# A long convolution and a segmented attention on one core: keys as eight token classes, paired taps in four blocks, gate factors as value columns, the memory's sum in PSUM, and a new order

## The chip, the cores and the metric

The kernel runs on one core of one Trainium2 chip. The metric is the device time of one execution in microseconds (us), as the median of several. A profile is one execution, taken apart instruction by instruction. The engines are TensorE (PE, whose weight loads are listed apart as PEld), VectorE (DVE), ScalarE (ACT) and GpSimd (POOL); SyncE (SP) issues nearly all DMAs, in the order of its program.

## The reference

Two independent layers read their own inputs, and their outputs stand side by side in a [2048, 1280] result.

Layer A works on 2048 tokens and 640 channels. The key is filtered along the tokens with four taps per channel, the result is multiplied by the value, convolved causally with a filter as long as the sequence, and multiplied by the query:

```
k_shift = sum over t of k_pad[:, t:t + S, :] * shift_k[:, 3 - t]
kv = k_shift * v
y = causal convolution of kv with ssm_k (by FFT), + kv * ssm_D
a = q * y
```

Layer B projects x with three 640 x 640 matrices to 32 heads of 20 columns and works on four segments of 512 tokens in turn. In each, causal softmax attention inside the segment is mixed, by a gate per head, with a read from a memory that earlier segments wrote:

```
a_dot = softmax(qs @ ks.T * scale + mask) @ vs
a_mem = phi(qs) @ M / (phi(qs) @ z + 1e-6)
o = g * a_mem + (1 - g) * a_dot,  with g = sigmoid(beta)
M = M + phi(ks).T @ vs;  z = z + sum of phi(ks)
```

The output is `o @ wo`. phi(t) is t + 1 above zero and exp(t) below.

## The kernel before

**Layer A** is five blocks of 128 channels (`conv(dp)`). A block loads its long filter (`load_filter`), loads and filters the key (`short_filter`), takes both through a transform made of matmuls with the table Wf (`spectrum`, whose PSUM results are copied to the tile F and combined on DVE), multiplies the two spectra on DVE (`product`), and goes back with the table Wi (`inverse`). The tokens stand as eight classes: token 8p + e of a half of 1024 tokens is row p of class e.

The short filter runs on PE. The key block is turned (channels on partitions) by one DMA transpose from DRAM into the tile kr, 16 zero columns ahead of 2048 tokens. The weights of each matmul are 128 of its columns, eight apart (`kr[:, first + m:first + m + 1017:8]`), and the moving operand skd is a matrix with the taps on its diagonal. Blocks 0 and 1 do it with seven matmuls of up to 512 columns for each of four results. Blocks 2 to 4, listed in `TAP2`, pair two taps: with three more DMAs (the step "lc"), kr and a second tile kb each hold 64 channels twice, the second time shifted by two tokens, and ten matmuls of 128 or 64 columns do.

**Layer B** is eight units u: four segments s, each in two halves of 16 heads. `project(u)` makes queries and keys (KQ), turns them by DMA (KQT), makes the values (Va), phi of both (PP, for the queries in two steps of two token tiles each), a bound for the logits that stands in for the row maximum (the tiles kam, A, qabs, bT), and adds the segment to the memory Mbd. `attend(u)` makes the masked logits on PE in four kinds of fills (A, D, J: two exponentials of 128 x 1024 on ACT for each, into ET), and `values` multiplies them with Va. Every head's slot has 22 columns; column 20 of Va holds 1 + exp(beta), so that the column's sum is the softmax's denominator with the factor of the gate in it. Memory's own denominator is multiplied by 1 + exp(-beta) in another way: the update goes through a mask into the tile mt, its column 20 is multiplied by emg, and mt is added to Mbd, three DVE instructions in all. `project_out(s)` multiplies the segment's outputs with wo and stores them.

**The order** is no loop's. `Recorder` collects each operation of the whole program (1543 of them; the matmuls of one PSUM result count as one), and two packed lists at the end of the file, ORDER and BASE, give the sequence in which they are issued and the PSUM bank of each result. Each engine, and SP, runs its part of this list in order and waits on semaphores. All instructions are issued at line 256. `EVICT` says for each of the 238 copies out of PSUM whether ACT or DVE does it. At the start, 20 matmuls on zeros (`WARM`) keep PE busy while the first loads are under way.

Of the kernel before, what the change touches and what calls it, by code (L numbers as in the profile page):

```python
# [13 lines left out]
bf16 = mybir.dt.bfloat16  # L14
f32 = mybir.dt.float32
# [29 lines left out]
def small_consts():  # L45
# [3 lines left out]
    sel = np.zeros((128, 32), np.float32)  # L49
# [4 lines left out]
    for hh in range(4):  # L54
        rows = (hl == hh) & (d < DH)
        maskbd[rows, hh, 0:DH + 1] = 1.0
        epsrow[32 * hh + DH + 1, hh] = EPS
# [207 lines left out]
class Layer:  # L265
    def __init__(self, ctx, tc, A_q, A_k, A_v, A_shift_k, A_ssm_k, A_ssm_D, B_x, B_wq, B_wk, B_wv, B_wo, B_beta, out):
# [14 lines left out]
        self.rings = {}  # L281
# [30 lines left out]
        skr = self.ring("skd", [128, 4, 128])[0:5].rearrange("c a b -> c (a b)")  # L312
# [31 lines left out]
        self.evict(self.taps[:], tp, g)  # L344

# [4 lines left out]
        self.kr = c.tile([128, KPAD + S], bf16, name="kr")  # L350
# [6 lines left out]
        nc.gpsimd.memset(self.kr[:, 0:KPAD], 0.0)  # L357
        self.kb = c.tile([128, KPAD + S], bf16, name="kb")
        nc.gpsimd.memset(self.kb[:, 0:KPAD], 0.0)
# [7 lines left out]
        if WARM:  # L367
# [4 lines left out]
            for n in range(WARM):  # L372
                rec.key = ("warm", n)
                with rec.one():
                    nc.tensor.matmul(g.ap[:, 0, 0:WARMC], lhsT=idle[:, 0:128], rhs=idle[:, 128:128 + WARMC], start=True, stop=True, grp=g)

# [19 lines left out]
    def beta_setup(self):  # L396
        nc, c, bt = self.nc, self.consts, self.bt
        V = nc.vector
        em = c.tile([128, H], f32, name="em")
# [3 lines left out]
        nc.scalar.activation(out=em[:], in_=g.ap[:, 0, 0:H], func=ACTF.Exp, scale=-1.0, grp=g)  # L403
        ep, ginv = [self.ring("rr", [128, 2, 16], f32, n=2)[:].rearrange("p a b -> p (a b)") for _ in range(2)]
        nc.scalar.activation(out=ep, in_=g.ap[:, 0, 0:H], func=ACTF.Exp, grp=g)
        omginv = c.tile([128, H], f32, name="omginv")
        V.tensor_scalar(out=em[:], in0=em[:], scalar1=1e30, scalar2=None, op0=ALU.min)
        V.tensor_scalar(out=ginv, in0=em[:], scalar1=1.0, scalar2=None, op0=ALU.add)
        V.tensor_scalar(out=omginv[:], in0=ep, scalar1=1.0, scalar2=1e30, op0=ALU.add, op1=ALU.min)
        for h in range(2):  # L410
            V.tensor_copy(out=self.Va[h][:, :, :, DH], in_=omginv[:, None, 16 * h:16 * h + 16].to_broadcast([128, 4, 16]))
        self.emg = em[:].rearrange("p (g h) -> p g h", h=4)
        for h in range(2):
            V.tensor_tensor(out=self.Mbd[h][0][:, :, :, DH], in0=ginv[:, 16 * h:16 * h + 16].rearrange("p (g h) -> p g h", h=4),
                            in1=self.epsrow[:, None, :].to_broadcast([128, 4, 4]), op=ALU.mult)

# [11 lines left out]
    def conv(self, dp):  # L428
# [31 lines left out]
        def short_filter():  # L460
            key("lk")
            kr = self.kr
            if dp in KTURN:
                kn = self.ring("ET", [128, 4, 512], n=ETBUF)[:].rearrange("p (b c) (e d) -> p (b c) e d", c=2, e=4)[:].rearrange("p x e d -> p (x e) d")
                for a in range(2):
                    nc.sync.dma_start(out=kn[:, 8 * a:8 * a + 8], in_=self.k[1024 * a:1024 * a + 1024, dsl].rearrange("(p e) d -> p e d", e=8))
                for x in range(4):
                    key("kn", x)
                    g = self.group(1, "kn")
                    with rec.one():  # L470
                        for e in range(4):
                            nc.tensor.matmul(g.ap[:, 0, 128 * e:128 * e + 128], lhsT=kn[:, 4 * x + e], rhs=self.ident[:], start=True, stop=True, grp=g)
                    at = KPAD + 1024 * (x // 2)
                    self.evict(kr[:, at:at + 1024].rearrange("d (p e) -> d e p", e=8)[:, 4 * (x % 2):4 * (x % 2) + 4], g.ap[:, 0, :].rearrange("d (e p) -> d e p", e=4), g)
            else:
              nc.sync.dma_start_transpose(out=kr[:, KPAD:KPAD + S], in_=self.k[:, dsl])
            if dp in TAP2:
# [8 lines left out]
            key("skd")  # L486
            skd = self.ring("skd", [128, 4, 128])
            if dp in TAP2:
                skd2 = skd[:].rearrange("p a d -> p (a d)")[:, 0:256].rearrange("p (f l d) -> p f l d", f=2, l=2)
                V.tensor_tensor(out=skd2, in0=self.id2[:, None, None, :].to_broadcast([128, 2, 2, 64]), in1=self.taps[:, 0:4, dp].rearrange("p (f l) -> p f l", f=2)[:, :, :, None].to_broadcast([128, 2, 2, 64]), op=ALU.mult)  # L490
            else:
                V.tensor_tensor(out=skd[:], in0=self.ident[:, None, :].to_broadcast([128, 4, 128]),
                                in1=self.taps[:, 4:8, dp, None].to_broadcast([128, 4, 128]), op=ALU.mult)
# [471 lines left out]
```

## Time and profile before

| | |
|---|---|
| time, median of 3 runs | 272.57 us (272.38 to 272.6) |
| profiled execution, first to last instruction | 272.0 us |
| PE busy | 260.8 us, 96% |
| PE weight loads busy | 195.4 us, 72% |
| DVE busy | 250.9 us, 92% |
| ACT busy | 248.8 us, 91% |
| DMA packets | 43.74 MB in 126972 packets |

The time outside the span, 0.57 us against the median, is what lies around the profiled instructions and the difference between two executions. Matmuls are pipelined, so a busy PE may still have room; "busy" counts a stretch once where two instructions overlap. The mean duration of a group is that of an instruction by itself, from its start to its end.

### The profile page before, as it was taken

The page shows a single profiled execution, that of the slowest core. Times are in us where ns is not written, and L with a number is a line of the kernel's source. Part 1 is how long each engine was busy: PE and PEld are TensorE (multiplying, and loading weights), DVE is VectorE, ACT ScalarE, POOL GpSimd, SP SyncE. Part 2 cuts the span into 40 slices and gives each one's busy share as a digit, 9 for nine tenths or more (in the row PEclk, how much of TensorE's full clock was granted, in tenths as well). Part 3 has the DMA queues.
Part 4 walks back from the last instruction along what each step waited for, and adds up shares of the span by engine and source line. Part 5 has one row for each costly group of instructions (what it writes and reads, how often), then busy time and mean ns, then how long its engine had stood idle before and what let it go on. Part 6 is the DMA issues. An engine that isn't in the chain of part 4 may idle for free.

```text
span 272.0 us, 10130 instructions
## 1 busy us (share of the span) xinstructions
PE 260.8 (96%) x4368; PEld 195.4 (72%) x4371; DVE 250.9 (92%) x424; ACT 248.8 (91%) x388; POOL 6.9 (3%) x18
## 2 busy tenths in 40 slices
PE   8999999999998999999999999999999989999995
PEld 3879777868766677878676787768677765756783
DVE  0599999999999999999999999999999998999972
ACT  1586799999999999999999999999999998999962
POOL 9100000000000000000000000000000000000000
PEclk9999999999999999999999999999999997999999
DMA  6999399999989599998979599994974081894024
GB/s 166 347 207 243 82 191 225 311 194 172 170 217 201 144 195 195 191 178 159 159 165 190 116 151 226 147 197 65 146 177 82 4 154 27 169 155 90 27 68 133
DMA packets 126972, 43.74 MB, mean 161 GB/s; under 512 B 117339, under 2 KB 124512, under 8 KB 126800
## 3 DMA queue, kind: packets, MB, share of 16 engines
q1 hardware_dynamic: 126768, 42.91, 79.9%
q8 instruction: 34, 0.56, 0.9%
q0 software_dynamic: 160, 0.20, 0.2%
q14 instruction: 10, 0.08, 0.1%
HBM read 14.12 MB, written 7.34 MB: 79 GB/s over the span
## 4 chain that ended last, share of the span: by engine, by line
PE 55%; ACT 33%; issue 6%; DVE 4%; ACTq 0%; DVEq 0%
PE ps L256 55%; ACT ET L256 21%; ACT F L256 4%; ACT KQ L256 3%; ACT PP L256 3%; ACT outb L256 1%; ACT Va L256 1%; DVE F L256 1%; DVE pq L256 1%; DVE Kh L256 1%; ACT bT L256 1%; DVE qabs L256 0%; DVE vt L256 0%; DVE Xh L256 0%; DVE PP L256 0%
## 5 line engine op out<-in xcount | busy, mean ns | idle before, releaser
L256 ACT ACTIVATE ET<-ps 128x1024 bf16<-128x1024 f32 x160 | 160.6, 1102 | 1.9 <-PE ps L256 1.7
L256 PE MATMUL ps<-wqkv,xT 128*128 128x320 bf16 x480 | 76.3, 300 | 0.5 <-ACT ET L256 0.3
L256 PEld LDWEIGHTS <-xT 128*128 128x128 bf16 x640 | 58.1, 98 | 25.7 <-issue 5.2
L256 PE MATMUL ps<-Va,ET 128*128 128x21 bf16 x1280 | 42.4, 172 | 0.3 <-ACT ET L256 0.3
L256 ACT CAST F<-ps 128x512 bf16<-128x512 f32 x69 | 42.0, 687 | 0.3 <-PE ps L256 0.3
L256 PEld LDWEIGHTS <-ET 128*128 128x128 bf16 x1280 | 39.7, 96 | 3.0 <-issue 2.2
L256 PE MATMUL ps<-KQT 32*128 32x128 bf16 (+2 forms) x896 | 34.6, 240 | 1.1 <-ACT ET L256 1.0
L256 PEld LDWEIGHTS <-Wf 128*128 128x128 bf16 x320 | 28.9, 97 | 6.1 <-issue 1.5
L256 ACT CAST KQ<-ps 128x320 bf16<-128x320 f32 x61 | 28.2, 496 | 1.4 <-PE ps L256 1.3
L256 PE MATMUL ps<-wo,xT 128*128 128x320 bf16 x160 | 25.4, 299 | 0.0
L256 PEld LDWEIGHTS <-KQT 32*128 32x128 bf16 x896 | 16.0, 92 | 10.9 <-issue 9.9
L256 PE MATMUL ps<-vt,Wf 128*128 128x256 bf16 x160 | 22.4, 272 | 0.1
L256 PE MATMUL ps<-kT,Wf 128*128 128x256 bf16 x160 | 22.2, 273 | 0.2 <-ACT ET L256 0.2
L256 PE MATMUL ps<-Y,Wi 128*128 128x256 bf16 x160 | 21.7, 280 | 0.0
L256 DVE TENSOR_TENSOR o<-ps,rr 128x640 bf16<-128x640 f32 x24 | 19.5, 814 | 0.2
L256 PE MATMUL ps<-Mbd,PqT 128*128 128x84 bf16 x96 | 18.1, 202 | 1.2 <-ACT ET L256 0.9
L256 DVE TENSOR_TENSOR Y<-Y,pq 128x2048 bf16<-128x2048 bf16 (+1 forms) x20 | 18.6, 945 | 0.0
L256 DVE TENSOR_TENSOR pq<-Xh,Kh 128x2048 bf16<-128x2048 bf16 x15 | 18.1, 1209 | 0.0
L256 PEld LDWEIGHTS <-Wi 128*128 128x128 bf16 x160 | 15.3, 100 | 3.5 <-issue 1.0
L256 ACT ACTIVATE PP<-KQ 128x640 bf16<-128x640 bf16 (+1 forms) x18 | 17.7, 991 | 0.0
L256 PE MATMUL ps<-pack 32*128 32x128 bf16 x512 | 14.7, 216 | 1.9 <-ACT ET L256 1.7
L256 ACT CAST Va<-ps 128x320 bf16<-128x320 f32 x31 | 15.0, 520 | 1.2 <-PE ps L256 1.2
(93 smaller groups left out, 370.0 us busy)
## 6 DMA issues: line engine op xcount, KB each, us to landing
vt<-in_A_v_dram SPq DMA_DIRECT2D x10, 256.0 KB
pq<-in_A_q_dram SPq DMA_DIRECT2D x10, 256.0 KB
out_dram<-outb SPq DMA_DIRECT2D x13, 160.0 KB
turned<-kT SPq DMA_DIRECT2D x4, 512.0 KB
kT<-turned SPq DMA_DIRECT2D x8, 256.0 KB
out_dram<-pq SPq DMA_DIRECT2D x8, 256.0 KB
kb<-kr SPq DMA_DIRECT2D x6, 256.0 KB
Wf<-c_wf SPq DMA_DIRECT2D x4, 256.0 KB
```

What stands on the lines that cost most here:

```text
L256: f(*[fix(a) for a in args], **{k: fix(v) for k, v in kw.items()})
```

## The change

- **Keys.** kr and kb become [128, 8, 16 + 256] tiles: class e of the eight, then its tokens. In the `TAP2` blocks the key is loaded into kb as it lies in DRAM (two DMAs), turned from there into kr by two DMA transposes inside the chip, and paired by five copies instead of three. The weights of a matmul are then 128 columns that lie side by side. Block 0 keeps the transpose from DRAM and its strided weights.
- **Paired taps** in blocks 1 to 4. The tap matrices of blocks 0 to 2 are made at the start (`filter_weights`), the ring skd has two smaller tiles.
- **Gate.** Va has column 0 for 1 + exp(beta) and column 21 for 1 + exp(-beta), the values stand in columns 1 to 20. The memory's denominator is column 21.
- **Memory's sum.** A further matmul, of the identity with the old Mbd, adds it to the update in PSUM; one DVE instruction masks the sum into the new Mbd.
- **Smaller steps.** phi of the queries in one step of four tiles; the tile A with 4 columns instead of 32 per group; in the first segment two groups of heads share a reciprocal and a multiply; the final add writes runs of 80.
- **Lists.** `WARM` is 10, `EVICT` gives 38 copies to DVE instead of 31, and ORDER and BASE are new, with 1510 operations.

```diff
-            V.tensor_copy(out=self.Va[h][:, :, :, DH], in_=omginv[:, None, 16 * h:16 * h + 16].to_broadcast([128, 4, 16]))
+            some = og[:, :, 16 * h:16 * h + 16]
+            V.tensor_copy(out=self.Va[h][:, :, :, 0:VW:DH + 1], in_=some.rearrange("p i h -> p h i")[:, None].to_broadcast([128, 4, 16, 2]))
...
         def short_filter():
...
-              nc.sync.dma_start_transpose(out=kr[:, KPAD:KPAD + S], in_=self.k[:, dsl])
...
+            flat = kb[:].rearrange("p e n -> p (e n)")
+            if dp in TAP2:
                 for a in range(2):
+                    rows = flat[:, 1024 * a:1024 * a + 1024]
+                    nc.sync.dma_start(out=rows.rearrange("p (e d) -> p e d", e=8), in_=self.k[1024 * a:1024 * a + 1024, dsl].rearrange("(p e) d -> p e d", e=8))
+                for a in range(2):
+                    key("kx", a)
+                    nc.sync.dma_start_transpose(out=kr[:, :, KPAD + 128 * a:KPAD + 128 * a + 128], in_=flat[:, 1024 * a:1024 * a + 1024])
                 key("lc")
                 q = self.queue("lc", dp)
-                q.dma_start(out=self.kb[64:128, KPAD:KPAD + S], in_=kr[64:128, KPAD:KPAD + S])
-                q.dma_start(out=self.kb[0:64, KPAD:KPAD + S], in_=kr[64:128, KPAD - 2:KPAD + S - 2])
-                q.dma_start(out=kr[64:128, KPAD:KPAD + S], in_=kr[0:64, KPAD - 2:KPAD + S - 2])
+                q.dma_start(out=kb[64:128], in_=kr[64:128])
+                q.dma_start(out=kb[0:64, 2:8], in_=kr[64:128, 0:6])
+                q.dma_start(out=kb[0:64, 0:2, KPAD - 1:], in_=kr[64:128, 6:8, KPAD - 2:-1])
+                q.dma_start(out=kr[64:128, 2:8], in_=kr[0:64, 0:6])
+                q.dma_start(out=kr[64:128, 0:2, KPAD:], in_=kr[0:64, 6:8, KPAD - 1:-1])
...
+            def tokens(kx, a, e):
+                at = KPAD + 128 * a - (e < 0)
+                return kx[:, e % 8, at:at + 128]
...
-            for i, n in ((0, 4), (1, 2)):
+            for i, n in ((0, 4), (1, 4)):
...
-        A = self.ring("A", [128, 4, 32], n=1)
+        A = self.ring("A", [128, 4, 4], n=1)
...
-                        nc.tensor.matmul(pmv[:, k, :, 0:DH + 1], lhsT=PP[:, 0, t, 4 * k:4 * k + 4, :], rhs=Va[:, t, 4 * k:4 * k + 4, 0:DH + 1],
-                                         start=(t == 0), stop=(t == 3), grp=g)
-            mt = self.ring("mt", [128, 4, 4, VW])
-            V.tensor_tensor(out=mt[:, :, :, 0:DH + 1], in0=pmv[:, :, :, 0:DH + 1], in1=self.maskbd[:, None, :, 0:DH + 1].to_broadcast([128, 4, 4, DH + 1]), op=ALU.mult, grp=g)
-            V.tensor_tensor(out=mt[:, :, :, DH], in0=mt[:, :, :, DH], in1=self.emg[:, 4 * half:4 * half + 4, :], op=ALU.mult)
-            V.tensor_tensor(out=dst[:, :, :, 0:DH + 1], in0=src[:, :, :, 0:DH + 1], in1=mt[:, :, :, 0:DH + 1], op=ALU.add)
+                        nc.tensor.matmul(pmv[:, k, :, 1:VW], lhsT=PP[:, 0, t, 4 * k:4 * k + 4, :], rhs=Va[:, t, 4 * k:4 * k + 4, 1:VW],
+                                         start=(k == 0 and t == 0), stop=False, grp=g, skip_group_check=True)
+                nc.tensor.matmul(pmv[:, :, :, 1:VW], lhsT=self.ident[:], rhs=src[:, :, :, 1:VW], start=False, stop=True, grp=g, skip_group_check=True)
+            V.tensor_tensor(out=dst[:, :, :, 1:VW], in0=pmv[:, :, :, 1:VW], in1=self.maskbd[:, None, :, 1:VW].to_broadcast([128, 4, 4, DH + 1]), op=ALU.mult, grp=g)
...
+        def values(pp, parts):
+            for j in range(2):
+                if s or not j:
+                    g = self.group(2, "o")
+                weighted(2 * pp + j, *parts[j], g, 0 if s else j)
+                if s == 0 and j == 0:
+                    continue
...
-WARM, WARMC = 20, 512
+WARM, WARMC = 10, 512
...
-TAP2 = (2, 3, 4)
+TAP2 = (1, 2, 3, 4)
```

What the new lists move, read from them. **Start:** SP loads one tile of x ahead of the long filter of block 0, which came first before; seven of the ten matmuls on zeros stand ahead of the first turning of that filter (18 of 20 before), the other three between the transforms that follow. **SP:** 198 DMAs instead of 181; in each paired block the loads of the key stand 1 to 14 places ahead of its transposes, and these up to 14 places ahead of the copies. **EVICT:** DVE takes three more copies of values, two more of KQ, two more of the last turning, one more of the output, and one less of F; the last eight output copies are all DVE's (three before). **End:** the last logits, the last inverse transforms and the 24 last output steps stand as before.

More of the change, by code (lines that the diff above doesn't have):

```diff
@@ L461, in short_filter @@
             key("lk")
-            kr = self.kr
-            if dp in KTURN:
-                kn = self.ring("ET", [128, 4, 512], n=ETBUF)[:].rearrange("p (b c) (e d) -> p (b c) e d", c=2, e=4)[:].rearrange("p x e d -> p (x e) d")
+            kr, kb = self.kr, self.kb
+            flat = kb[:].rearrange("p e n -> p (e n)")
+            if dp in TAP2:
                 for a in range(2):
[L466 to L475, printed above, removed]
-              nc.sync.dma_start_transpose(out=kr[:, KPAD:KPAD + S], in_=self.k[:, dsl])
@@ L485, in short_filter @@
             self.halves(self.queue("lv", dp), vt, self.v, dsl)
[L486 to L493, printed above, removed]
+            if dp not in self.skd:
+                self.filter_weights(dp)
+            skd = self.skd[dp]
             for b in range(4):
                 key("ks", b)
[L496 to L498 removed]
+                w = KSW[dp]
+                if b % w == 0:
+                    g = self.group(w, "ks")
+                ps = g.ap[:, b % w, :]
                 if dp in TAP2:
```

169 lines of the change are left out of this document (92 added, 77 removed).

## The prediction

> **What bounds the kernel now.** I read the page's busy line first, then the busy time by stretches, then the chain of work that ended last.
>
> ```profile
> span 272.0 us, 10130 instructions
> PE 260.8 (96%) x4368; PEld 195.4 (72%) x4371; DVE 250.9 (92%) x424; ACT 248.8 (91%) x388; POOL 6.9 (3%) x18
> PE 55%; ACT 33%; issue 6%; DVE 4%; ACTq 0%; DVEq 0%
> ```
>
> ```profile
> 0.00:20.00 20.00, 18.69 (x148) 12.74 (x150) 9.85 (x18) 11.06 (x21) 6.94 (x18) 1.00 0.94 240
> 20.00:256.00 236.00, 229.56 (x4013) 172.98 (x4014) 232.16 (x392) 229.29 (x356) 0.00 (x0) 0.99 0.84 159
> ```
>
> The columns of the second fence are the stretch, its length, busy time and instructions of PE, PEld, DVE, ACT and POOL, the granted clock, the DMA share and GB/s. From 20 to 256 us three engines are all full: DVE 232.2 of 236 us (98%), ACT 97%, PE 97%. None of them alone is the bound, and no wait of any length is left to take away. So the question is how much work each loses, and whether the first 20 us, where DVE and ACT are half empty, get longer. The chain runs over PE and ACT for 88% and over DVE for 4%, though DVE is as full.
>
> **What an instruction costs.** A mean duration is not what an engine gives up for it. Four neighbours on DVE (start, duration):
>
> ```profile
> 220.38 0.68 DVE L256 CAST F<-ps 128x512 bf16<-128x512 f32 x1
> 220.98 0.68 DVE L256 TENSOR_TENSOR Xh<-Xh 128x1024 bf16<-128x1024 bf16 x1
> 221.58 0.35 DVE L256 RECIPROCAL rr<-ps 128x32 f32<-128x32 f32 x1
> ```
>
> They start 0.60 us apart and last 0.68: each begins 0.08 us before the one ahead of it has ended. I take duration less 0.08 us for every DVE instruction. For ACT the chain of waits gives the same (start, length, what):
>
> ```profile
> 65.86 1.15 ACT PP L256
> 91.09 0.65 ACT KQ L256 x2
> 91.74 0.33 ACT Va L256
> 158.25 0.61 ACT PP L256
> 158.87 0.48 ACT F L256
> ```
>
> So a copy of F costs ACT 0.48 us, one of KQ or Va 0.33, phi of two tiles 0.61 and of four 1.15.
>
> **The change part by part: DVE.** The rows of the groups (busy us, mean ns):
>
> ```profile
> L256 DVE TENSOR_TENSOR o<-ps,rr 128x640 bf16<-128x640 f32 x24 | 19.5, 814 | 0.2
> L256 DVE RECIPROCAL rr<-ps 128x32 f32<-128x32 f32 x24 | 8.4, 352 | 1.3 <-ACT ET L256 0.9
> L256 DVE TENSOR_TENSOR PP<-PP,qabs 128x640 bf16<-128x640 bf16 x12 | 5.7, 474 | 0.0
> L256 DVE TENSOR_TENSOR PP<-PP,qabs 128x1280 bf16<-128x1280 bf16 x6 | 4.9, 816 | 0.0
> L256 DVE TENSOR_TENSOR o_s<-ps,rr 128x320 bf16<-128x320 f32 x8 | 3.8, 474 | 0.0
> L256 DVE TENSOR_SCALAR qabs<-KQ 128x640 bf16<-128x640 bf16 x12 | 3.7, 308 | 0.0
> L256 DVE TENSOR_SCALAR qabs<-KQ 128x1280 bf16<-128x1280 bf16 x6 | 2.9, 483 | 0.0
> L256 DVE TENSOR_TENSOR A<-pack,kam 128x128 bf16<-128x128 bf16 x8 | 2.2, 273 | 0.0
> L256 DVE TENSOR_TENSOR Mbd<-Mbd,mt 128x336 bf16<-128x336 bf16 x6 | 2.0, 325 | 0.0
> L256 DVE RECIPROCAL rr<-ps 128x16 f32<-128x16 f32 x8 | 1.8, 240 | 0.2 <-PE ps L256 0.2
> L256 DVE CAST KQ<-ps 128x320 bf16<-128x320 f32 x3 | 1.4, 479 | 0.0
> L256 DVE TENSOR_TENSOR skd<-ident,taps 128x512 bf16<-128x512 bf16 x2 | 1.4, 679 | 0.0
> L256 DVE TENSOR_TENSOR mt<-mt,em 128x16 bf16<-128x16 bf16 x6 | 1.3, 212 | 0.0
> ```
>
> - Memory, six times: the multiply by em and the add to Mbd go: 6 x (0.212 + 0.325 - 2 x 0.08) = 2.3 us less. The masking multiply stays.
> - phi of the queries, twelve steps become six of double size. Multiply by the rows: 12 x 0.308 - 6 x 0.483 and 12 x 0.474 - 6 x 0.816 make 0.8 + 0.8, less 12 starts that were overlapped (1.0): 0.6 us less.
> - First segment, eight pairs of reciprocal and multiply become four: 8 x (0.240 + 0.474) - 4 x (0.352 + 0.814) - 8 x 0.08 = 0.4 us less.
> - A: 16 elements wide instead of 128; by the row of mt and em, which is 16 wide, 8 x (0.273 - 0.212) = 0.5 us less. The tap matrix of block 1 is half as wide: about 0.3 us less. The setup of the gate loses two instructions in the first 20 us, where DVE waits anyway: nothing.
> - Seven more copies: one of F fewer (0.60), six 320 wide more (6 x 0.40), two 512 wide more (2 x 0.60): 3.0 us more.
>
> DVE together: 4.1 less and 3.0 more, **1.1 us less**.
>
> **ACT.** Phi: 12 x 0.61 - 6 x 1.15 = 0.4 us less. Copies: one of F more (0.48), six 320 wide fewer (6 x 0.33) and two 512 wide fewer (2 x 0.48): 2.5 less. Together **2.9 us less**.
>
> **PE.** Weights of strided columns against those that lie together, seven-tap results against ten-matmul ones, and the rate at full clock:
>
> ```profile
> L256 PEld LDWEIGHTS <-ET 128*128 128x128 bf16 x1280 | 39.7, 96 | 3.0 <-issue 2.2
> L256 PEld LDWEIGHTS <-kr 128*128 128x128 bf16 x116 | 14.4, 149 | 1.7 <-issue 0.2
> ```
>
> ```profile
> 19.60 3.70 PEld L256 LDWEIGHTS <-kr 128*128 128x128 bf16 x28
> ```
>
> ```profile
> 117.15 0.28 PE L256 MATMUL ps<-skd,kr 128*128 128x128 bf16 x1
> ...
> 118.51 0.29 PE L256 MATMUL ps<-KQT 32*128 32x256 bf16 x4
> ```
>
> ```profile
> 15.61 3.96 PEld L256 LDWEIGHTS <-xT 128*128 128x128 bf16 x30
> ```
>
> Four seven-tap results take 3.70 us, 0.92 each. Two paired ones take from 117.15 to 118.51, 0.68 each. Thirty matmuls of 320 columns take 3.96 us, 0.41 ns a column, and a paired result has 1024 columns: 0.42 us, with ten starts perhaps 0.45. The difference up to 0.68 is what the strided loads (149 ns against 96) cost. Now block 1 goes from 0.92 to 0.45, four times (1.9 us less), blocks 2 to 4 from 0.68 to 0.45, twelve times (2.8 less), and the memory's sum adds 336 columns six times (0.8 more): **3.8 us less**. If the loads stayed slow, block 1 alone would gain (1.0) and it would be 0.1 less; that is the other end.
>
> The ten matmuls on zeros that go lie in time that PE waits for loads.
>
> **The middle's sum** lies between DVE's 1.1 and ACT's 2.9 us. Because the chain names PE and ACT for 88%, I take 2.5 us less. A new order can win or lose some more; I see no row for it, and keep 2 us to either side.
>
> **DMA and SP.** Each paired block's key now moves through DRAM to kb, then to kr: 2048 packets of 256 bytes more for each of four blocks, and block 1 gets the copies.
>
> ```profile
> q1 hardware_dynamic: 126768, 42.91, 79.9%
> ```
>
> ```profile
> 48.00:72.00 24.00, 24.00 (x441) 19.25 (x439) 23.68 (x44) 24.00 (x42) 0.00 (x0) 1.00 1.05 209
> ```
>
> ```profile
> SPq L256 <- PE ps L256: 45.1, 19, 9.2
> ```
>
> 79.9% of 272 us over 42.91 MB is 5.1 us a MB of all 16 engines' time; four blocks of 0.52 MB and 0.79 MB for block 1's copies are 2.9 MB or 15 us, on 217. I cost it at nothing: PE, DVE and ACT are full even in the stretch whose DMA share is 1.05 (second last column), and SP, which waited 45 us for PE alone, has room for 17 more issues. What hides it is that the loads of a block stand ahead of their use by tens of microseconds. Without that cover it is the last rival below.
>
> **The head.** DVE and ACT wait there for the first transforms. The long filter is now SP's second load, one issue later, and only seven matmuls on zeros run ahead of its first use.
>
> ```profile
> 5.07 0.15 PEld L256 LDWEIGHTS <-o 128*128 128x128 bf16 x1 [0.28 <-issue]
> 5.50 1.42 PEld L256 LDWEIGHTS <-o 128*128 128x128 bf16 x7 [0.28 <-issue]
> 7.04 0.73 PEld L256 LDWEIGHTS <-kT 128*128 128x128 bf16 x8
> ```
>
> Until 5.5 us the zeros' matmuls start 0.43 us apart, after it 0.20: full clock came after ten of them. In the same trace it went away once more:
>
> ```profile
> 220.60:224.00 3.40, 2.33 (x75) 1.75 (x72) 3.37 (x6) 3.40 (x6) 0.00 (x0) 1.00 0.98 170
> 224.00:227.40 3.40, 3.40 (x25) 1.94 (x23) 2.91 (x4) 2.11 (x3) 0.00 (x0) 0.50 0.20 33
> ```
>
> After 3.4 us in which PE worked 2.33, the granted clock is 0.50 for 3.4 us; ACT loses 1.3 us in it. Seven matmuls end at about 1.3 + 7 x 0.43 = 4.3 us, then PE stands still until the filter lands. At best nothing is lost, and the first turning, which stood behind 18 of the zeros, even starts 0.5 us earlier; at worst the clock rises only after 4.3 us of work from the first turning on, at 7.0 us, and half of these 4.3 us, 2.2, is lost. The loads that the first transforms wait for hide some of it. I take 0.7 us more, nearer to the good end; the filter's place one issue later is small beside these ends.
>
> The Trainium skill (TensorE: Matmul & The Clock Gate, Part 1) says that PE starts at half clock, gets the full one after some 3.4 us of sustained work, and falls back after an idle window of that length. The trace's 4.3 us of work before the change agrees; its fall at 224 us came after a window that was one third idle, which is less than the page asks. By the page seven matmuls (3.0 us) are too few, the first 3.4 us of real work run at half rate, an estimate of 1.7 us more instead of my 0.7, and the whole sum would be 1.0 us higher.
>
> **Sum.** 272.0 - 2.5 + 0.7 = 270.2 us of span; the median stood 0.6 above the span: **270.8 us**.
>
> **The rivals.**
>
> 1. *All savings arrive.* ACT's 2.9 us come in full, DVE's surplus fits its 3.8 us of idle time in the middle, the half clock at 224 us doesn't return (1.3 less) and the head keeps its length: 272.6 - 2.9 - 1.3 = 268.4 us. For it: ACT and PE, the chain's engines, both lose about 3 us. Against: DVE is at 98% and loses least.
> 2. *The head stays at half clock.* Seven matmuls are 3.0 us of work where the clock came after 4.3, so turning and transforms run at half rate: 2.2 us more at the head, 2.5 less in the middle: 272.6 - 2.5 + 2.2 = 272.3 us, no change. For it: the rows at 5.07 and 5.50; against: what the loads hide. It is the mechanism of the Trainium skill's section named above.
> 3. *The keys' longer way costs, and it is slower.* The place is the DMA engines between 20 and 192 us, where all of the added 15 us fall (0.09 of share). The busiest stretch stands at 1.05; if that is all they can do, the 24 us of this stretch, and by an estimate as much again elsewhere, get longer by 0.09 / 1.05, 4.1 us, since the turned keys and queries of the attention stand in the same queue: 272.6 - 2.5 + 0.7 + 4.1 = 274.9 us. It decides from the point where the turned keys land later than PE wants them. Against it: no wait of PE for a DMA stands in the chain before.
>
> **How the numbers follow.** The forecast has 0.46, the rivals 0.22, 0.17 and 0.15. The forecast's own range, with the order's 2 us, is 268.8 to 272.8. The range of 267.0 to 274.5 takes in rivals 1 and 2 and stops short of rival 3. A measurement of this kernel tells 0.2%, 0.55 us, from no change: 272.0 and 273.1 are the borders. Faster: rival 1's 0.22, 0.39 of the forecast and 0.02 of rival 2, together 0.63. Same: 0.06 of the forecast and 0.12 of rival 2, 0.18. Slower: 0.01 of the forecast, 0.03 of rival 2 and rival 3's 0.15, 0.19.
>
> **What would show it.** Right: paired results about 0.45 us apart on PE and loads of kr and kb near 96 ns; DVE busy in the middle shorter by about 1 us, ACT by about 3; the chain still over PE and ACT; DVE's first transform instruction within 1 us of its old start. Rival 2: zeros and first transforms at 0.43 us a 512-column matmul beyond 8 us. Rival 3: PE or DVE waiting for DMA into kr, kb or KQT. Wrong would be a DVE busy time that doesn't fall, or a sum that falls while new idle time takes its place.

## The result, and the profile after

The changed kernel takes 285.72 us (median of 4 runs, 284.75 to 287.59) where the kernel before takes 272.56. The ratio is 1.0486, with a 95% interval of 1.0447 to 1.0525: 13 us slower, where 270.8 us was predicted. An execution more than 1.5% above the fastest one of its kernel counts as slow, and the medians below leave such executions out.

The page of the changed kernel, its span, busy, packet and queue lines:

```profile
span 283.7 us, 10132 instructions
...
PE 260.9 (92%) x4377; PEld 193.5 (68%) x4379; DVE 254.6 (90%) x397; ACT 246.8 (87%) x375; POOL 7.2 (3%) x18
...
DMA packets 136620, 46.78 MB, mean 165 GB/s; under 512 B 125771, under 2 KB 133968, under 8 KB 136448
...
q1 hardware_dynamic: 136416, 45.96, 82.8%
```

PE is as busy as before (260.8), ACT 2 us less, DVE 3.7 us more although it has 27 instructions fewer. The span is 11.7 us longer, so all three now stand idle. The page's chain reaches back only to 228.9 us here, 18% of the span, so it can't tell whether PE and ACT still carry it. The queue's share of the 16 DMA engines rose from 79.9% of 272.0 us to 82.8% of 283.7, from 217 to 235 us of their time: 18 us, near the 15 that the prediction counted. It is good to some us only: the same product is 231, 235 and 237 us in three runs with the changed kernel's DMAs.

Where the idle time lies is seen in three stretches (columns as in the prediction's windows). The kernel before:

```profile
20.00:72.00 52.00, 51.88 (x755) 40.95 (x757) 51.44 (x88) 47.37 (x85) 0.00 (x0) 1.00 0.97 197
72.00:120.00 48.00, 45.94 (x828) 35.03 (x828) 47.24 (x81) 47.39 (x72) 0.00 (x0) 1.00 0.97 192
120.00:256.00 136.00, 131.74 (x2436) 97.00 (x2434) 133.48 (x225) 134.53 (x202) 0.00 (x0) 0.99 0.74 133
```

The changed kernel:

```profile
20.00:72.00 52.00, 48.10 (x738) 36.50 (x736) 48.28 (x74) 45.00 (x78) 0.00 (x0) 1.00 0.95 201
72.00:120.00 48.00, 43.45 (x751) 31.90 (x740) 42.12 (x59) 43.33 (x63) 0.00 (x0) 0.93 1.09 194
120.00:256.00 136.00, 129.09 (x2355) 95.59 (x2354) 131.23 (x211) 132.65 (x200) 0.00 (x0) 1.00 0.81 148
```

From 20 to 120 us DVE was idle for 1.3 us (100 less 51.44 and 47.24); now it is idle for 9.6. From 120 to 256 us it went from 2.5 to 4.8. So most of the loss falls into the stretch whose DMA share (second last column) was 0.97 before and is 0.95 and 1.09 now.

What the engines waited for, by the waits of the changed kernel (total us, times, longest):

```profile
PEld L257 <- DMA kr<-kr: 5.9, 4, 2.3
...
PE ps L257 <- DMA KQT<-bT: 3.8, 2, 2.2
...
PE ps L257 <- DMA kr<-kr: 3.0, 3, 1.4
```

These name the last copy of the pairing, and the rows of the logits' bound. The waits of the kernel before name no DMA for PE, DVE or ACT. SyncE (SP), which issues the DMAs, stood 2.9 us for landings before, the last stores left out. Now it is 19.7 us. Four of its rows are:

```profile
SPq L257 <- DMA kb<-kr: 7.3, 4, 4.2
...
SPq L257 <- DMA pq<-in_A_q_dram: 3.8, 1, 3.8
...
SPq L257 <- DMA kb<-in_A_k_dram: 2.7, 2, 2.4
...
SPq L257 <- DMA kr<-kb: 2.6, 2, 1.9
```

The longest of them, and what it leads to, in the timelines of SP and of PE (start, length):

```profile
35.38 2.06 SPq L257 DMA_DIRECT2D kb<-kr  x3
37.48 0.59 SPq L257 DMA_DIRECT2D turned<-kT  x1
42.37 0.46 SPq L257 DMA_DIRECT2D kr<-kr  x1
...
44.06 0.68 SPq L257 DMA_DIRECT2D kr<-kr  x1
```

```profile
43.90 0.40 PE L257 MATMUL ps<-KQT 32*128 32x256 bf16 x8
46.33 0.23 PE L257 MATMUL ps<-skd,kr 128*128 128x128 bf16 x1 [2.03 <-ACT ET L257]
...
46.83 0.25 PE L257 MATMUL ps<-Va,ET 128*128 128x21 bf16 x4
47.44 0.23 PE L257 MATMUL ps<-skd,kr 128*128 128x128 bf16 x1 [0.36 <-DMA kr<-kr]
...
47.90 0.45 PE L257 MATMUL ps<-Va,ET 128*128 128x21 bf16 x12
```

The copies into kb read what the copies into kr overwrite, so SP stood from 38.1 to 42.4 us until the former had landed. The filter of block 1 started only at 46.33, after 2.03 us in which PE ran nothing; the row names an exponential, but the weight load of the same moment waited 2.31 us and names the copy kr<-kr, issued at 44.06. The paired results themselves are as fast as predicted: 46.33 to 46.83 and 47.44 to 47.90, 0.50 and 0.46 us.

### The profile page after: what moved, and what is told of

Its sections match the earlier page's. It is cut to its first block, busy times and chain, and to the rows that moved or that the text cites. A ratio compares the mean times of both kernels' runs of the same rounds, so it can differ in the third digit from the quotient of the medians.

```text
span 283.7 us, 10132 instructions
## 1 busy us (share of the span) xinstructions
PE 260.9 (92%) x4377; PEld 193.5 (68%) x4379; DVE 254.6 (90%) x397; ACT 246.8 (87%) x375; POOL 7.2 (3%) x18
## 3 DMA queue, kind: packets, MB, share of 16 engines
q1 hardware_dynamic: 136416, 45.96, 82.8%
## 5 line engine op out<-in xcount | busy, mean ns | idle before, releaser
L257 ACT ACTIVATE ET<-ps 128x1024 bf16<-128x1024 f32 x160 | 165.4, 1134 | 8.3 <-PE ps L257 8.2
L257 PEld LDWEIGHTS <-xT 128*128 128x128 bf16 x640 | 59.8, 98 | 29.7 <-issue 7.5
L257 ACT CAST F<-ps 128x512 bf16<-128x512 f32 x70 | 42.7, 701 | 3.3 <-PE ps L257 3.3
L257 PEld LDWEIGHTS <-ET 128*128 128x128 bf16 (+1 forms) x1292 | 39.4, 96 | 4.2 <-issue 3.1
L257 PE MATMUL ps<-Va,ET 128*128 128x21 bf16 x1280 | 41.6, 173 | 0.4 <-ACT ET L257 0.4
L257 PEld LDWEIGHTS <-KQT 32*128 32x128 bf16 x896 | 16.8, 93 | 14.5 <-issue 13.3
L257 DVE TENSOR_TENSOR o<-ps,rr 128x640 bf16<-128x640 f32 x24 | 19.7, 820 | 0.6
L257 DVE TENSOR_TENSOR vt<-ps,vt 128x512 bf16<-128x512 f32 x20 | 13.1, 685 | 4.8 <-PE ps L257 2.8
L257 ACT ACTIVATE PP<-KQ 128x1280 bf16<-128x1280 bf16 x12 | 16.2, 1388 | 0.7 <-DMA PqT<-PP 0.7
L257 ACT CAST Va<-ps 128x320 bf16<-128x320 f32 x28 | 14.4, 529 | 2.1 <-PE ps L257 2.1
## 6 DMA issues: line engine op xcount, KB each, us to landing
kb<-kr SPq DMA_DIRECT2D x4, 272.0 KB
```

Of the source, the lines that this page charges most:

```text
L257: f(*[fix(a) for a in args], **{k: fix(v) for k, v in kw.items()})
```

## The experiments

Four theories were tested. **B:** the DMA engines are full in the first half, and every added MB makes other transfers late. **Q:** SP stands for landings, and what it issues next comes late. **O:** the new order is bad in itself. **H:** the half clock that follows the stalls costs the time. Ratios are against the kernel before, run on the same chip beside each; its median there lay between 272.75 and 273.49 us.

**Keys the old way, in the new order.** Blocks 1 to 4 turn their key from DRAM again.

```diff
-                for a in range(2):
-                    nc.sync.dma_start_transpose(out=kr[:, :, KPAD + 128 * a:KPAD + 128 * a + 128], in_=flat[:, 1024 * a:1024 * a + 1024])
+                nc.sync.dma_start_transpose(out=kf[:, KPAD:KPAD + S], in_=self.k[:, dsl])
```

> The changed kernel with the old way of the keys in blocks 1 to 4 (one transpose from DRAM, three copies, weights of strided columns), everything else and the order as changed. Theory Q (SP's queue: the longer chain of dependent key DMAs makes SP stand for landings, 19.7 us against 3, and what is queued behind lands late): at least half of the 13 us comes back, 272 to 279 us. Theory O (the new order is bad in itself, whatever the keys' way): 283 us or more. Theory B (the DMA engines are too full): all comes back, 271 to 274 us.

Measured: 279.5 us, ratio 1.0229 (1.0171 to 1.0287), 44.52 MB. SP's waits:

```profile
SPq L257 <- DMA kb<-kr: 8.1, 3, 5.3
```

About 6 of the 13 us go with the longer way of the keys. The rest stays, and SP still stands for the copies. The time lies between the ranges of Q and O, so this run decides for none of the three.

**The copies issued by GpSimd**, so that SP need not stand.

```diff
-BULK = ()
+BULK = ("lc",)
```

> The changed kernel with the five copies that pair the taps issued by POOL instead of SP, so that their waits for landings hold up nothing on SP; the same bytes and the same order otherwise. Theory Q: 275 to 281 us, SP's waits for DMA down from 19.7 to about 10 us. Theories O and B: 285 us, within 1.

Measured: 291.19 us, ratio 1.0648 (1.0586 to 1.071). Waits of this run:

```profile
POOL kb L257 <- DMA kr<-kb: 46.1, 1, 46.1
...
PEld L257 <- DMA kr<-kr: 4.2, 1, 4.2
PE ps L257 <- DMA kr<-kr: 3.9, 1, 3.9
PE ps L257 <- DMA kr<-kb: 2.3, 1, 2.3
```

SP is free of the copies (its waits for landings fell from 19.7 to 8.4 us), PE waits for them as before, and the kernel is slower still. Theory Q as put there fell: SP's standing is not what costs by itself. The copies now wait on GpSimd, 46.1 us at once, so the run doesn't clear the waits of one copy for another. The Trainium skill (DMA: Bandwidth & Descriptors, Issuing engines are not separate DMA queues) says that DMAs issued by any engine run on the same 16 DMA engines, and that another issuer saves only the issuing engine's own time. This run agrees in that nothing was saved (291.19 us after 285.72).

**The new keys in the old order**, blocks 2 to 4 only, with the small tile A to make room.

```diff
-             nc.sync.dma_start_transpose(out=kr[:, KPAD:KPAD + S], in_=self.k[:, dsl])
+                    nc.sync.dma_start(out=rows.rearrange("p (e d) -> p e d", e=8), in_=self.k[1024 * a:1024 * a + 1024, dsl].rearrange("(p e) d -> p e d", e=8))
...
+                    nc.sync.dma_start_transpose(out=kr[:, :, KPAD + 128 * a:KPAD + 128 * a + 128], in_=flat[:, 1024 * a:1024 * a + 1024])
```

> The kernel before with the new way of the keys in blocks 2 to 4 alone (two loads, two turns, five copies, weights that lie together), put into the old order at the places of the old transposes and copies; the tile A is made small too, to have room, which takes DVE about 0.7 us less. Theory Q: slower, 275 to 281 us, with SP waiting for landings. Theory O: 271 to 273 us. Theory B: 276 us or more without long waits of SP.

Measured: 280.32 us, ratio 1.0232 (1.0164 to 1.03), 45.43 MB. Its waits, and its second stretch:

```profile
PE ps L256 <- DMA KQT<-bT: 2.8, 1, 2.8
PEld L256 <- DMA xT<-in_B_x_dram: 2.4, 1, 2.4
PE ps L256 <- DMA xT<-in_B_x_dram: 2.1, 1, 2.1
```

```profile
72.00:120.00 48.00, 43.01 (x731) 31.87 (x730) 41.43 (x70) 43.55 (x66) 0.00 (x0) 0.96 1.02 188
```

The keys alone cost the old order about 7 us. PE waits for no key there but for what stands behind it in the queue, the rows of the bound and x, and DVE is idle for 6.6 of 48 us. DMAs, which the chain before didn't name, now make 10% of it:

```profile
PE 49%; ACT 29%; DMA 10%; issue 5%; DVE 3%; SPq 3%; ACTq 0%; DVEq 0%
```

**The rest in the old order**: gate columns, memory's sum in PSUM, one-step phi, small A, the old keys.

```diff
-            for i, n in ((0, 4), (1, 2)):
+            for i, n in ((0, 4), (1, 4)):
...
+                nc.tensor.matmul(pmv[:, :, :, 1:VW], lhsT=self.ident[:], rhs=src[:, :, :, 1:VW], start=False, stop=True, grp=g, skip_group_check=True)
```

> The kernel before, keys, taps, copies and order as they were, with the rest of the change: gate factors as value columns, the memory's sum in PSUM, phi of the queries in one step, the small tile A. By the sums of the prediction DVE has 3.3 us less and ACT 0.4 less, PE 0.8 more: all theories 270 to 272 us; 274 or more would mean that one of these parts costs what the change lost.

Measured: 275.17 us, ratio 1.0082 (1.0056 to 1.0107), though DVE is busy for 2 us less (248.8). Two more runs took it apart. The sum in PSUM, the gate columns and the small A without the one-step phi:

> The kernel before with the gate columns, the memory's sum in PSUM and the small A, without the one-step phi (with it: 275.2 us, ratio 1.008). If the memory's sum is what the prediction took it for: DVE loses 12 instructions of some 2 us in all, TensorE gains six matmuls, 271 to 272.5 us. If it costs (six more matmuls of 84 columns on a full TensorE, Va's column copies at the start): 274 to 275.5 us, and the one-step phi is neutral.

Measured: 273.57 us, ratio 1.0012 (0.9995 to 1.0028): no change. And the one-step phi alone, the first two lines of the diff above, with one transposing DMA for its result instead of two:

> The kernel before with phi of the queries in one step of four tiles and its transpose into PqT in one DMA, nothing else. All smaller edits together gave 1.0082, the sum in PSUM with the small A and the gate's columns 1.0012. If the one-step phi is the difference: 274.5 to 275.5 us. If the loss comes only when they are together: 272.5 to 273.5 us.

Measured: 275.71 us, ratio 1.0097 (1.0068 to 1.0125). So the one-step phi, placed where the second of the two steps stood, is the whole loss. The group of its exponentials on ACT:

```profile
L256 ACT ACTIVATE PP<-KQ 128x1280 bf16<-128x1280 bf16 x12 | 15.8, 1335 | 0.3 <-DMA PqT<-PP 0.3
```

ACT's work for it is less, as predicted. Against the kernel before, exponential by exponential, the delay grows in steps of 0.4 to 1.0 us between 60 and 218 us. That each step now begins only when all four token tiles are projected, and stands 1.3 us in front of the logits' exponentials, is a likely reason; its single DMA is another. No run here tells them apart.

**Zeros in the stalls.** Nine matmuls on zeros ahead of three stalled results of the changed kernel, to keep the clock up. Its longest stretch at half clock:

```profile
100.34:107.17 6.83, 6.23 (x80) 3.97 (x81) 3.62 (x5) 3.81 (x6) 0.00 (x0) 0.50 0.80 187
```

```diff
+                        if (dp, b) in ((1, 3), (2, 2)):
+                            self.zeros(ps, g)
```

> The changed kernel with nine matmuls on zeros (512 columns each, into the result's own bank, which the real matmuls then overwrite) at three places where PE stands: ahead of the fourth paired result of block 1, of the third of block 2, and of the joined logits of unit 2. If the half clock that follows these waits costs what a half rate of 6.8 us costs: 3 us less, 282 to 283 us, and no half clock near 100 us. If the clock matters little: 285 to 286 us.

Measured: 287.01 us, ratio 1.0494 (1.0433 to 1.0555); the half clock near 100 us is gone and the median is no lower. The profiled execution had a late start: its first exponential came at 37.28 us instead of 33.70. From there to the end it took 248.6 us, the changed kernel 250.0, so by this pair the half clock is worth 1.4 us, not 13. Theory H fell as the cause of the loss.

**More traffic in the old order.** Three loads of 256 KB behind each turned key of blocks 1 to 4, DRAM to DRAM; no operation reads them.

```diff
+              for j in range(3 if dp else 0):
+                  nc.sync.dma_start(out=self.spare[j][:].rearrange("(p e) d -> p e d", e=8), in_=self.k[1024 * a:1024 * a + 1024, dsl].rearrange("(p e) d -> p e d", e=8))
```

> The kernel before with three more loads of 256 KB in each of blocks 1 to 4 (rows of 256 bytes of the key, 3.1 MB in all, as much as the change adds), into scratch in DRAM that nobody reads, behind each block's transpose on SP. Theory B (the DMA engines are too full): 276 us or more. Theory Q: 272 to 274 us, since nothing waits for them.

Measured: 280.19 us against 273.34, ratio 1.0229 (1.0185 to 1.0272). Its queue line, stretches, waits and chain:

```profile
q1 hardware_dynamic: 139248, 46.05, 82.9%
```

```profile
20.00:72.00 52.00, 49.77 (x720) 38.81 (x719) 51.22 (x87) 45.66 (x81) 0.00 (x0) 1.00 1.06 210
72.00:120.00 48.00, 44.89 (x777) 33.77 (x777) 43.00 (x72) 45.02 (x68) 0.00 (x0) 0.96 0.94 201
```

```profile
PE ps L256 <- DMA KQT<-bT: 2.7, 1, 2.7
...
PEld L256 <- DMA spare<-in_A_k_dram: 1.9, 1, 1.9
...
PEld L256 <- DMA xT<-in_B_x_dram: 1.1, 1, 1.1
PE ps L256 <- DMA xT<-in_B_x_dram: 0.9, 1, 0.9
```

```profile
PE 53%; ACT 23%; DMA 9%; DVE 7%; issue 5%; SPq 1%; ACTq 0%; DVEq 0%
```

The last line is the chain, with 9% of DMAs in it. 82.9% of 278.4 is 230.8 us of the DMA engines' time, 13.5 more than the kernel before, and the kernel loses 6.9 by the medians (6.2 by the ratio). The waits for KQT and xT are those of the new keys in the old order. The loads were issued from 25.4, 47.3, 88.3 and 131.3 us. The order is that of the kernel before, so the two can be compared exponential by exponential: the run is 0.7 us ahead at the first, 3.5 behind after the wait for KQT near 72 us and the half clock that follows it, 4.3 behind after the wait for xT near 116, 5.9 at 138.2 (the 61st, 132.3 before) and 6.2 from 147 us to the end. So the last three loads cost up to 2 us too. The wait put down to a load itself (spare) stands there, at 137.77, ahead of logits whose rows were issued behind these loads; whether PE waited for the loads or for those rows isn't shown. Theory B is shown for the old order: loads that no operation reads cost more than 6 us.

Whether it is the issues or the volume was told by loads of 4 KB in their place:

```diff
-                  nc.sync.dma_start(out=self.spare[j][:].rearrange("(p e) d -> p e d", e=8), in_=self.k[1024 * a:1024 * a + 1024, dsl].rearrange("(p e) d -> p e d", e=8))
+                  nc.sync.dma_start(out=self.spare[j][:], in_=self.k[0:16, dsl])
```

> The kernel before with the same twelve further DMAs as the run that added 3.1 MB to it (three behind each key's transposing load in blocks 1 to 4, DRAM to DRAM, nobody waits for them), but each of 4 KB in 16 packets instead of 256 KB in 1024. Theory B: what costs is the time on the DMA engines, so this is at the kernel before, 272 to 273.5 us (the larger loads gave 280.2). If what costs is SP's time for issuing twelve more, or their places in the queue whatever their size: 277 to 280 us.

Measured: 274.12 us, ratio 1.0027 (0.9999 to 1.0055). Twelve more issues cost about 0.7 us or nothing. And by the same bytes in whole rows (`in_=self.k[0:205, :]`):

> The kernel before with the twelve further loads of 256 KB, DRAM to DRAM, as in the run that gave 280.2, but each of 205 whole rows that lie side by side, so in packets far larger than 256 B. If a packet costs time for itself (the twelve loads had 12480 packets of 256 B), the engines need less time and the kernel comes to 274 to 277 us. If the bytes cost: 279 to 281 us.

Measured: 273.12 and 276.2 us, 274.66 in the mean, against 273.49. The ratio on record, 1.0174 (1.0114 to 1.0234), is higher than these two give, 1.004, so the cost of these loads isn't settled. The queue line:

```profile
q1 hardware_dynamic: 127152, 46.06, 82.5%
```

82.5% of 271.3 us, the span of the profiled execution, is 223.8: the same 3.15 MB took 6.5 us of the engines instead of 13.5, in 384 packets instead of 12480. But five runs with the DMAs of the kernel before (two of them with 192 packets fewer) have 208.7 to 218.5 us, so the difference of 7 us is not clear of their spread, and neither of the two sizes is exact. The profiled execution (273.12) lost nothing by the loads, the other 2.7 us. The Trainium skill (DMA: Bandwidth & Descriptors, Why small descriptors are slow) gives 27% of overhead for 256 bytes from a fixed cost of each packet. The sign here is the same (230.8 against 223.8 us); no run here shows the size.

**Less traffic in the old order.** The three pairing copies left out, 2.4 MB.

```diff
-                q.dma_start(out=self.kb[64:128, KPAD:KPAD + S], in_=kr[64:128, KPAD:KPAD + S])
...
-                            for f, kx in ((0, kr), (1, self.kb)):
+                            for f, kx in ((0, kr), (1, kr)):
```

> The kernel before without its three pairing copies in blocks 2 to 4 (both shifts from kr, so the filtered key is not the reference's); about 2.3 MB of DMA less than the kernel before. Theory B in its strong form (the kernel before already waits for full DMA engines): 268 to 271 us. In its weak form (the kernel before is just under the knee, its orders having been fitted to its landings): 272 to 273 us, no change, since PE, DVE and ACT are full.

Measured: 273.03 us, ratio 1.0001 (0.9983 to 1.0019), with

```profile
q1 hardware_dynamic: 126048, 40.55, 75.6%
```

that is 204.8 of 270.9 us, 12.5 less. Nothing is won below the kernel before, and something is lost above it: 205, 217, 224 and 231 us of the DMA engines' time go with 273.0, 272.6, 274.7 and 280.2 us.

**The changed kernel without its copies**, both shifts from kr.

```diff
-                q.dma_start(out=kb[64:128], in_=kr[64:128])
...
-                q.dma_start(out=kr[64:128, 0:2, KPAD:], in_=kr[0:64, 6:8, KPAD - 1:-1])
```

> The changed kernel without the five copies that pair the key in blocks 1 to 4; its matmuls take both shifts from kr, so the filtered key is not the reference's, and the same number of matmuls of the same size runs. About 3.1 MB of DMA less than the changed kernel (46.78 MB), so about the volume of the kernel before (43.74 MB). Theory B (the DMA engines are full through the middle, and every added packet makes rows, turned keys and x land later): the changed order is as good as the old once the volume is back, 268 to 273 us, TensorE's waits for DMAs near 3 us in sum. Theory O (the new order of the instructions is bad in itself): 278 us or more, with the idle time of DVE in the middle as in the changed kernel. Theory Q (SP stands for landings of the copies) gives what B gives here, 268 to 273; the next run parts B from Q.

Measured: 277.87 us, ratio 1.0133 (1.0063 to 1.0202). The stretches, and the clock's windows in the head:

```profile
20.00:72.00 52.00, 51.30 (x767) 39.34 (x766) 51.17 (x80) 46.80 (x81) 0.00 (x0) 1.00 0.90 188
72.00:120.00 48.00, 46.85 (x827) 35.46 (x828) 46.72 (x69) 47.12 (x70) 0.00 (x0) 0.96 1.04 188
```

```profile
5.66:9.08 3.42, 1.59 (x20) 1.15 (x20) 0.60 (x1) 1.09 (x3) 2.35 (x5) 1.00 0.95 294
9.08:12.49 3.41, 3.41 (x29) 2.70 (x30) 0.71 (x2) 0.57 (x1) 0.00 (x0) 0.50 1.43 295
```

The time is near O's 278, and above the 268 to 273 of B. But DVE's idle time from 20 to 120 us is 2.1 us, nearly the 1.3 of the kernel before, where O has the 9.6 of the changed kernel. So the copies make the stalls there, and are worth 7.8 of the 13 us by the medians (9.6 by the ratios). Part of what is left lies in the head of this execution, where the clock fell to 0.5, DVE's first combination starts at 16.84 us instead of 14.57, and the first exponential at 36.7 instead of 33.7.

**Idle copies.** In place of the copies, at their places in SP's program, DMAs of about their bytes that wait for nothing and that nobody waits for.

```diff
-                q.dma_start(out=kb[64:128], in_=kr[64:128])
...
+                for j in range(5):
+                    r = (216, 162, 54, 162, 54)[j]
+                    q.dma_start(out=self.spare[j][0:r], in_=self.k[0:r, :])
```

> The changed kernel with its five pairing copies per block replaced, at the same places of SP's program, by five DMAs of about the same bytes (648 rows of 1280 B per block, 3.3 MB in all) from DRAM to DRAM that wait for nothing and that nobody waits for; both shifts are taken from kr, so the filtered key is not the reference's. Without any such DMAs the changed kernel took 277.9, with its own copies 285.7. Theory B (volume on full DMA engines): 282 to 286 us. Theory Q (SP standing for the landing of one copy before it issues the next, and TensorE waiting for the last of them): 277 to 279.5 us.

Measured: 281.28 us, ratio 1.0289 (1.0251 to 1.0327). Between the two: by the medians 3.4 us above the run without copies and 4.4 below the changed kernel (4.3 and 5.4 by the ratios). So in the new order the volume of the copies makes a little under half of their cost, as B has it, and the rest is their waits, at SP and at PE, as Q has it. The split is rough: by the queue lines the copies took some 16 us of the DMA engines' time and the idle ones some 10, so the volume's part may be larger.

**More zeros in the head** of the changed kernel, 17 instead of 7 ahead of the first turning.

```diff
-WARM, WARMC = 10, 512
+WARM, WARMC = 20, 512
```

> The changed kernel with 17 matmuls on zeros ahead of the first turning of the filter instead of 7, as many as the kernel before about. If the short row of zeros is what lets TensorE fall back to half clock in the head (the rival of the half clock in the head, worth 1.5 to 3 us in most executions): 283 to 284.5 us, and the first combination at 14 to 15 us after the start. If the head is set by the landings of the loads: 285 to 287 us as without.

Measured: 287.7 us, ratio 1.053 (1.05 to 1.056): no help. The clock didn't fall in its head, and the first combination still starts at 15.69 us. So more zeros are not what the head lacks.

**Constants in one late wait of the kernel before**, where the clock fell at 224 us.

```diff
+                if u == 6 and key == (1, "D"):
+                    for n in range(5):
+                        nc.tensor.matmul(gs[0].ap[:, 0, :], lhsT=self.ident[:], rhs=self.wo[:, 0, 0:512], start=True, stop=True, grp=gs[0], skip_group_check=True)
```

> The kernel before with five matmuls on constants ahead of the second set of diagonal logits of the seventh unit, where TensorE waited about 1.1 us near 222 us and the granted clock then fell to 0.5 for 3.4 us; the bank they write is overwritten from its start. If the wait causes the fall and the fall costs: no window of half clock near 224 us in the profile and 271.5 to 272.5 us, faster than the kernel before. If the fall costs nothing: no change.

Measured: 272.44 us against 272.75, ratio 0.9979 (0.9962 to 0.9997). The timeline of the kernel before and of this one:

```profile
222.10 0.23 PE L256 MATMUL ps<-pack 32*128 32x128 bf16 x2 [0.39 <-ACT ET L256]
223.02 0.40 PE L256 MATMUL ps<-pack 32*128 32x128 bf16 x14 [0.69 <-ACT ET L256]
```

```profile
221.56 1.24 PE L256 MATMUL ps<-wo,ident 128*128 128x512 bf16 x5 [0.39 <-ACT ET L256]
222.73 0.40 PE L256 MATMUL ps<-pack 32*128 32x128 bf16 x16
```

The five matmuls fill the 0.69 us, and no half clock follows in the profiled execution. It is the one version below the kernel before, by 0.2%, with an interval that ends just below 1.

## Why the prediction was wrong

- **The step that failed** is "I cost it at nothing", said of 15 us of added DMA time. Its size was near (18 us). Its cover wasn't there: that "the loads of a block stand ahead of their use by tens of microseconds" holds for the loads (block 1's are issued from 20.89 us on, its filter starts at 46.33), but turning and pairing follow them, each behind the landing of the one before. What counts is the last copy. In the new order it is issued 2.3, 4.7, 6.8 and 1.5 us ahead of the filters of blocks 1 to 4; in the kernel before it stood 9.2, 9.3 and 12.4 us ahead of those of blocks 2 to 4 (block 3's at 107.88, whose filter starts at 117.15). So in the changed kernel the key itself came late, and PE waited 8.9 us for it (the two rows for kr). Where the new keys kept 8.0 to 11.8 us, in the old order, rows and x behind them came late instead. A share of 0.97 before, with no wait of PE for a DMA, did not mean that there was room, as the runs with more traffic show. That copy of block 3 in the kernel before:

```profile
107.88 0.53 SPq L256 DMA_DIRECT2D kr<-kr  x1
```

- **The first rival**, all savings arriving, needed engines that stay full; they didn't. **The third** had the place and the mechanism, and its sign that was named for it (PE waiting for kr and KQT) appeared. Its price of 4.1 us was too small: 13.5 us of DMA time cost 6.9 us in the old order, and the copies 7.8 in the new one. It took the loss as the added share over one full stretch and as much again; but a wait of PE holds up DVE and ACT with it, and nothing is made up later (in the run with more traffic the delay stays at 6.2 us from 147 us on). What stood against it, that no wait for a DMA stands in the chain before, was weighed as evidence of room, and so it got 0.15.
- **SP** has room for 17 more issues: right as far as it went (twelve tiny ones cost about 0.7 us). Not counted were the copies that must wait for other copies to land, 7.3 us in which everything behind them stood.
- **PE's terms** were right for the paired results, 0.46 to 0.50 us each (0.45 predicted), with loads of kr at 97 ns, but its busy time did not fall by the 3.8 us (260.9 after 260.8); 10.2 us of it now ran at half clock, 3.4 before:

```profile
L257 PEld LDWEIGHTS <-kr 128*128 128x128 bf16 x80 | 7.1, 97 | 6.5 <-DMA kr<-kr 5.9 <-issue 0.2
```

- **DVE's and ACT's terms** were right too, and came to nothing. Counted from each instruction's start to the next one's, or to its own end where that is earlier, DVE's memory step lost 1.9 us (2.3 predicted), phi 0.5 (0.6), the first segment 0.3 (0.4), A 0.7 (0.5), and the added copies took 3.2 (3.0); ACT's copies and phi lost 3.4 (2.9). All other instructions of DVE together took about 4 us more: an instruction that begins after a gap has no 0.08 us of overlap with the one ahead, and 94 of DVE's begin so, 45 before; 49 times 0.08 is 3.9 us. In the run without copies it is 85, so most of this comes with the new order and not with the copies. This is why "DVE busy shorter by about 1 us" turned into 3.7 longer.
- **The middle's 2.5 us less** did not come even without the copies. From the first exponential to the last the kernel before takes 227.6 us (33.7 to 261.3) and the changed kernel without copies 229.4. Of the single edits the sum in PSUM gave nothing (1.0012), and the one-step phi, taken for 1.0 us less, cost 2.6 in the old order (1.0097). "2 us to either side" for the new order was too narrow.
- **The head's** 0.7 us lies inside what was seen, which is wide. In the profiled execution of the changed kernel the first combination came earlier than the 14.57 us of before:

```profile
13.87 1.23 DVE L257 TENSOR_TENSOR Kh<-F 128x2048 bf16<-128x2048 bf16 x1
```

  In the six other profiled runs of the new order, whose start is the same but for the zeros of one, it lies between 14.28 and 17.46 us; in the ten of the old order, the one before among them, between 13.83 and 15.19. The second rival, the half clock in the head, is seen in some of them (the windows from 5.66 us above), yet more zeros don't cure it. What sets this spread stays open; landings of the first tables are the nearest candidate, since PE waited 1.5 to 2.0 us for Wf in two of the slower ones.
- **The time outside the span** was set at 0.6 us from two different executions. In later runs the time and the span of the same execution lie 1.7 to 1.8 apart (280.2 and 278.4, 273.04 and 271.3). So the profiled span of 272.0 belongs to an execution of about 273.8 us, slower than the timed ones, and the forecast of the median should have been 1.2 us higher.

Counted from the first exponential to the end of the span, which leaves the head out, the profiled executions take 238.3 us (before), 250.0 (changed), 240.7 (changed, without copies) and 244.4 (with idle copies). Of the 11.7 us between the first two, 9.3 go with the copies, 3.7 of them with the idle ones' volume; by the medians the copies are 7.8. The other 2.4 stay with the new order, where the prediction had 2.5 less. The one-step phi's 2.6 is known in the old order alone, so what makes up these 2.4 stays open. Each of these is a single execution.

## What to carry to other kernels

A kernel whose DMA share is near 1.0 in a stretch may have no room there even when nothing waits for a DMA. Here added loads cost about half of the DMA engines' time they took, by making late what stood behind them in the queue; as an estimate from this one case, that is a price to start from. A copy that must wait for another copy's landing blocks all that is issued behind it, so ask of each added DMA what it waits for, and how far ahead of its use the last of such a chain is issued. An edit that saves work on an engine can cost time in an order that was not made for it (the one-step phi): test it alone in the old one first.

## What the runs showed of the hardware

- The time that the DMA engines spend on the same DMAs differs between executions: 214.3, 217.3 and 218.5 us in three runs with the DMAs of the kernel before, 231.3, 234.9 and 236.7 in three of the changed kernel. Differences of a few us between single executions mean little.
- The clock falls to 0.5 after windows of some 3.4 us in which TensorE was far from idle: 2.33 of 3.40 us in the kernel before, 1.59 of 3.42 in the run without copies. The Trainium skill (TensorE: Matmul & The Clock Gate, Part 1) has it fall after an idle window of that length; the length agrees, the windows were half and two thirds busy.
- One such fall near 224 us cost 1.3 to 1.5 us: in the profiled executions of the old order without it (tiny loads, whole rows, no copies, constants) the exponentials behind it come that much sooner against the kernel before than those ahead of it, near the 1.3 that the prediction read. The median gained less by the constants (0.9979), since not every execution has the fall: beside these runs 23 executions of the kernel before with a mean clock of 1.0 took 272.6 us in the mean, 35 with 0.992 or 0.993 took 273.5.
- In the old order 12.5 us less of the DMA engines' time gave 1.0001, and 13.5 us more in packets of 256 B gave 1.0229.
